# The second MLP's first matrix product in seven block products for eight, its weights prepared step by step behind the first MLP's activations

## The chip, the cores and the metric

The kernel runs on one core of one Trainium2 chip. The metric is the device time of one execution in microseconds (us), the median of several runs. Five engines run side by side, each through its own list of instructions in order: TensorE (PE; PEld is its loading of weights), VectorE (DVE), ScalarE (ACT), GpSimd (POOL) and SyncE (SP), which here issues nearly all transfers (DMAs).

## The reference, cut to what matters

```python
attn_out = _attn_ref(q, k, v, M_prev, z_prev, beta)        # 4 batches, 8 heads, 576 rows, 64 columns
x = attn_out.transpose(0, 2, 1, 3).reshape(2304, 512)      # 2304 tokens
h = x @ moe_w_in                                           # first MLP: 512 -> 2048
x = where(h > 0, h, exp(min(h, 0)) - 1) @ moe_w_out        # ELU, 2048 -> 512
h = x @ moe2_w_in                                          # second MLP: 512 -> 2048
out = maximum(0.01 * h, h) @ moe2_w_out                    # leaky ReLU, 2048 -> 512
```

The weights reach the kernel as 64-bit floats, read as pairs of 32-bit integers.

## The kernel before

**Precision.** PE multiplies numbers of reduced width, so every factor x is held as two parts: the rounded high part `xh` and the rest `xl = x - xh`. A product is the sum of three: high by high, the weights' low by high, high by low. ACT or DVE makes the high part by a rounding copy, POOL (now and then DVE) the low part by a subtraction.

**Stages.** First the attention, with the first MLP's work on hidden blocks 0 to 6 (of 16 blocks of 128 hidden columns) woven into it. Then the rest of the first MLP, hidden blocks 7 to 15, over five token tiles (four of 512, the last of 256); I call it the first MLP's second half. Then the second MLP over the same five tiles.

**The first MLP's second half.** For each tile and each hidden block f: 12 matmuls give the hidden block in a bank of PSUM (`h_mm`, line 621; two banks named `pm` and two named `tp` take turns), `elu` (lines 633 to 635, then `g_split`, lines 243 and 628) passes through ACT twice, DVE twice and POOL once, and 12 matmuls (`o_mm`, line 649) two blocks later add its part of the output, held in four banks named `sc` and `po`. At a tile's end DVE adds the part made beside the attention (line 902) and the result goes to the DRAM scratch `x1_scr`.

**The second MLP's weights.** `load_w` makes one hidden block's weights: two fetches of 0.5 MB, the unpacking of 64-bit floats (ACT line 127, DVE lines 128, 129, 132, each over 128x1024 elements), the rounding copy (ACT line 241) and two subtractions (POOL line 138). A list `w2` holds the sixteen; two per tile are taken from it in tiles 1 to 4 of the first MLP's second half, the others are emitted behind that stage.

**The second MLP.** `load3` fetches a tile's input from `x1_scr` and splits it (ACT, POOL line 840). Each hidden block has 12 matmuls of 512 columns (line 621), `leaky` (ACT line 640, DVE line 641, then `g_split`), and two blocks later 12 matmuls into the output banks (line 919). At a tile's end DVE copies the four output banks in eight halves through two buffers named `st` (line 953), each sent out by its own DMA (line 954). All sixteen blocks' weights stay in SBUF.

**Order.** The code is emitted in this order, but a scheduler with a timeline model of its own sets each engine's list. `tc.issue_after` holds an instruction behind another, and a tile's buffer can be written anew only when its last reader is done.

## Time and profile before

| | us |
|---|---|
| median of 3 runs (1069.12 to 1070.02) | 1069.39 |
| profiled execution | 1069.05 |
| its span, first to last instruction | 1067.2 |
| PE busy in the span | 1040.3 |
| DVE busy | 591.8 |
| POOL busy | 531.6 |
| ACT busy | 485.2 |

The times are of one execution taken by the profiler; the span leaves out 1.85 us around the first and last instruction. Busy shares are averages over stages with different limits, so the stages are read one by one. A matmul's duration in the rows overlaps the next one's; its real cost is the distance between starts.

### The profile page before, as it was taken

The page shows a single profiled execution, that of the slowest core. Times are in us where ns is not written, and L with a number is a line of the kernel's source. Part 1 is how long each engine was busy: PE and PEld are TensorE (multiplying, and loading weights), DVE is VectorE, ACT ScalarE, POOL GpSimd, SP SyncE. Part 2 cuts the span into 40 slices and gives each one's busy share as a digit, 9 for nine tenths or more (in the row PEclk, how much of TensorE's full clock was granted, in tenths as well). Part 3 has the DMA queues.
Part 4 walks back from the last instruction along what each step waited for, and adds up shares of the span by engine and source line. Part 5 has one row for each costly group of instructions (what it writes and reads, how often), then busy time and mean ns, then how long its engine had stood idle before and what let it go on. Part 6 is the DMA issues. An engine that isn't in the chain of part 4 may idle for free.

```text
span 1067.2 us, 17324 instructions
## 1 busy us (share of the span) xinstructions
PE 1040.3 (97%) x5904; PEld 909.9 (85%) x5904; DVE 591.8 (55%) x1380; ACT 485.2 (45%) x1171; POOL 531.6 (50%) x674
## 2 busy tenths in 40 slices
...
GB/s 183 195 150 112 160 142 96 139 166 142 115 128 164 90 113 337 147 223 168 227 232 85 119 1 138 158 119 1 80 1 1 60 20 1 8 33 1 1 40 20
DMA packets 150120, 115.05 MB, mean 108 GB/s; under 512 B 80016, under 2 KB 141456, under 8 KB 150032
## 3 DMA queue, kind: packets, MB, share of 16 engines
...
q8 instruction: 47, 0.77, 0.3%
q14 instruction: 41, 0.34, 0.1%
...
## 4 chain that ended last, share of the span: by engine, by line
PE 80%; DVE 7%; DMA 4%; ACT 3%; issue 2%; POOL 2%; SPq 1%; DVEq 0%; POOLq 0%; ACTq 0%
PE pm L621 18%; PE sc L919 14%; PE tp L621 14%; PE sc L649 7%; PE pm L649 5%; PE po L919 4%; PE tp L457 4%; PE po L524 4%; PE pm L524 2%; PE po L649 2%; PE sc L426 2%; PE sc L428 1%; PE sc L429 1%; POOL w L138 1%; DMA wraw<-in_moe_w_in_dram 1%
## 5 line engine op out<-in xcount | busy, mean ns | idle before, releaser
L628 POOL TENSOR_TENSOR gl<-e,gh 128x512 fp32r<-128x512 f32 (+2 forms) x181 | 200.4, 1111 | 371.9 <-DVE gh L243 267.8
L621 PE MATMUL tp<-xw,w 128*128 128x512 f32 (+1 forms) x504 | 144.6, 367 | 1.7 <-DVE e L635 1.7
L621 PE MATMUL pm<-xw,w 128*128 128x512 f32 (+1 forms) x496 | 142.7, 369 | 1.2 <-ACT w L241 1.2
L919 PE MATMUL sc<-w,gh 128*128 128x512 f32 x448 | 135.9, 390 | 0.0
L451 POOL TENSOR_SCALAR pt<-pt,rs,omg 128x128 f32<-128x128 f32 (+4 forms) x160 | 104.1, 660 | 21.2 <-DVE rs L446 17.2
L621 PEld LDWEIGHTS tp<-xw,w 128*128 128x128 f32 x504 | 91.8, 188 | 18.3 <-DVE e L635 2.2
L621 PEld LDWEIGHTS pm<-xw,w 128*128 128x128 f32 x496 | 90.5, 188 | 17.7 <-ACT w L241 1.6
L436 ACT ACTIVATE pt<-pt,mx 128x128 f32<-128x128 f32 (+4 forms) x160 | 93.3, 585 | 23.2 <-DVE mx L431 21.6
L649 PE MATMUL sc<-gh,w 128*128 128x512 f32 (+2 forms) x438 | 103.2, 340 | 0.2 <-DVE gh L243 0.2
L919 PEld LDWEIGHTS sc<-w,gh 128*128 128x128 f32 x448 | 83.2, 188 | 16.5
L621 PE MATMUL tp<-xv,w 128*128 128x512 f32 (+1 forms) x252 | 92.6, 367 | 0.0
L621 PE MATMUL pm<-xv,w 128*128 128x512 f32 (+1 forms) x248 | 91.4, 369 | 0.0
L640 ACT ACTIVATE e<-pm 128x512 f32<-128x512 f32 (+1 forms) x40 | 22.2, 555 | 144.7 <-PE pm L621 141.7
L138 POOL TENSOR_TENSOR w<-wm,w 128x512 fp32r<-128x512 f32 x50 | 65.8, 1337 | 43.4 <-ACT w L241 39.4
L457 PE MATMUL tp<-ident,pt 128*128 128x128 f32 x480 | 82.0, 276 | 3.0 <-DVE al L250 1.5
L641 DVE TENSOR_TENSOR e<-tp,e 128x512 f32<-128x512 f32 (+1 forms) x40 | 25.5, 637 | 106.8 <-ACT e L640 106.8
L919 PE MATMUL sc<-w,gl 128*128 128x512 f32 x224 | 84.3, 389 | 0.0
L649 PEld LDWEIGHTS sc<-gh,w 128*128 128x128 f32 x438 | 74.6, 188 | 9.1 <-DVE gh L243 0.6
L641 DVE TENSOR_TENSOR e<-pm,e 128x512 f32<-128x512 f32 (+1 forms) x40 | 25.5, 637 | 102.1 <-ACT e L640 102.1
L621 PE MATMUL pm<-xh,w 128*128 128x288 f32 x368 | 79.6, 302 | 1.7 <-ACT xh L610 1.6
L243 DVE CAST gh<-e 128x512 fp32r<-128x512 f32 (+2 forms) x146 | 71.0, 490 | 13.5 <-PE po L919 3.0
L640 ACT ACTIVATE e<-tp 128x512 f32<-128x512 f32 (+1 forms) x40 | 22.2, 554 | 117.4 <-PE tp L621 117.4
...
## 6 DMA issues: line engine op xcount, KB each, us to landing
wraw<-in_moe_w_in_dram SPq DMA_DIRECT2D x32, 512.0 KB, 3.9
wraw<-in_moe_w_out_dram SPq DMA_DIRECT2D x32, 512.0 KB, 4.8
...
x<-x1s SPq DMA_DIRECT2D x9, 512.0 KB, 3.8
...
```

What stands on the lines that cost most here:

```text
L138: nc.gpsimd.tensor_tensor(out=w[:, 1, a], in0=t[:, a], in1=_f(w)[:, 0, a], op=ALU.subtract)
L243: (nc.vector if eng == "V" else nc.gpsimd).tensor_copy(dst, src)
L436: nc.scalar.activation(out=pt[0:m, 0:nk], in_=pt[0:m, 0:nk], func=AF.Exp, scale=-1.0, bias=mx[0:m, last:last + 1], accum_out=self.pd["ss"] ...
L451: nc.gpsimd.tensor_scalar(out=pt, in0=pt, scalar1=rs[0:m, i:i + 1], scalar2=omg[0:m, h:h + 1], op0=ALU.mult, op1=ALU.mult,)
L457: nc.tensor.transpose(dst, self.p[c][:, k0:k0 + kn], ident)
L524: nc.tensor.matmul(po[:, a:b], w, x, start=i == 0, stop=i == len(mms) - 1)
L621: nc.tensor.matmul(ph, wi[:, wj, kc, :], xx[:, kc, :], start=n_mm == 0, stop=n_mm == 11)
L628: nc.gpsimd.tensor_tensor(out=gl, in0=g, in1=_f(gh), op=ALU.subtract)
L640: nc.scalar.mul(t, ph, 0.01)
L641: nc.vector.tensor_tensor(out=t, in0=ph, in1=t, op=ALU.max)
L649: nc.tensor.matmul(py, wo[:, wj, ec * P:(ec + 1) * P], gg, start=opens and f == first and n_mm == 0, stop=closes and f == last and n_mm == 2,)
L919: nc.tensor.matmul(pos[tb], gg[:, tb * P:(tb + 1) * P], wo[:, wj, :], start=f == 0 and n_mm == 0, stop=f == NF - 1 and n_mm == 2,)
```

## The change

The first product of the second MLP, for tiles of 512 tokens, is cut into 2 x 2 blocks: for two hidden blocks (a pair, 256 columns) the weights into A11, A12, A21, A22 (256 inputs by 128 hidden columns each) and the tile's input into B11, B12, B21, B22 (256 inputs by 256 tokens). Instead of eight block products, seven are made (`product`, line 1115: six matmuls of 256 columns each), from A11, A12, A22, four sums of weight blocks (S1 to S4) and seven input blocks (B11, B21, B22, T1 to T4). Their results are added on DVE (`add`, line 1121), in two buffers `c0` and `c1` named `e`; then come the leaky ReLU on DVE (line 1125), the rounding copy on ACT (line 1128) and the low part on POOL (line 834). The 256-token tile keeps the old product.

The weight blocks are made in 33 steps, one behind each ELU of the first MLP's second half, from tile 0 on: per pair the unpacking, the split of the A blocks, the DVE sums, the split of the S blocks, and the same for the second matrix. All is written to DRAM scratch (`wa_scr`, `ws_scr`, `wo_scr`); pairs 0 and 1 also stay in SBUF, pair 4 is fetched early, the rest at the end of that stage. In the second MLP five pairs' A and S blocks fit in SBUF, so three pairs' blocks (2 MB each) are fetched again for each tile (`load_pair`), and the pairs are taken forwards and backwards in turn. The input blocks T1 to T4 are made on DVE when a tile of the first MLP ends, and the first tile's seven blocks are fetched and split during the last tile of the first MLP (`fetch_first`, `split_first`).

```diff
+    def decode(raw, m=None):
+        rw = raw.rearrange("p a n t -> p (a n) t")
+        lw, hw = rw[:, :, 0], rw[:, :, 1]
+        if m is None:
+            m = pools["wst"].tile([P, 2 * DM], I32, tag="wm", bufs=pools["nwm"], name="wm")
+        nc.scalar.activation(out=_f(m), in_=_f(hw), func=AF.Copy, scale=2.0 ** -112)
+        nc.vector.tensor_scalar(out=m, in0=m, scalar1=3, scalar2=None, op0=ALU.logical_shift_left)
+        nc.vector.scalar_tensor_tensor(
+            out=m, in0=lw, scalar=29, in1=m, op0=ALU.logical_shift_right, op1=ALU.bitwise_or
+        )
+        nc.vector.scalar_tensor_tensor(
+            out=m, in0=hw, scalar=-(1 << 31), in1=m, op0=ALU.bitwise_and, op1=ALU.bitwise_or
+        )
+        return _f(m)
...
+    x1_scr = [dram.tile([P, 7 if t + TW <= NT else 2, 2, TW // 2], F32, name=f"x1s{t}") for t in range(0, NT, TW)]
+    NPR = NF // 2
+    NKEEP = 2
+    wa_scr, ws_scr, wo_scr = (
+        [dram.tile([P, 4, 2, 2 * P], F32, name=f"{nm}{i}") for i in range(NPR)] for nm in ("wa", "ws", "wo")
+    )
...
+        pools["elu"] = [hi.ins, lo.ins]
...
+    def sub_lo(out, full, hi):
+        nc.gpsimd.tensor_tensor(out=out, in0=full, in1=hi, op=ALU.subtract)
...
+    def stage():
+        nonlocal n_stage
+        n_stage += 1
+        return n_stage % (NFA - 1)
...
+    def fetch_raw(key):
+        kind, pr = key
+        raw = raws[key] = raw_tile()
+        for j in range(2):
+            f = 2 * pr + j
+            if kind == "in":
+                dst = raw[:, j].rearrange("p (c n) t -> p c (n t)", c=NKC)
+                src = w2i[:, f * 2 * P:(f + 1) * 2 * P].rearrange("(c p) n -> p c n", p=P)
+            else:
+                dst, src = raw[:, j].rearrange("p n t -> p (n t)"), w2o[f * P:(f + 1) * P, :]
+            nc.sync.dma_start(dst, src)
...
+    def unpack(key, ahead):
+        m = None
+        if key[0] == "out":
+            m = w_tile(wpa, NFA - 1).rearrange("p a b n -> p (a b n)")[:, 0:2 * DM].bitcast(I32)
+        full[key] = decode(raws.pop(key), m)
+        if ahead:
+            fetch_raw(ahead)
...
+    SLOTS = [("a", 2, 3), ("a", 4, 5), ("b", 0, 1), ("b", 3, 4), None]
...
+    def split_in(pr, half):
+        t = full["in", pr].rearrange("p (k n) -> p k n", k=4)
+        v = as_blocks(w_tile(wpa, SLOTS[pr][1 + half] if pr < NKEEP else stage()))
+        nc.scalar.copy(v[:, :, 0], t)
+        for k in (0, 2):
+            sub_lo(v[:, k:k + 2, 1], t[:, k:k + 2], _f(v)[:, k:k + 2, 0])
+        nc.sync.dma_start((ws_scr if half else wa_scr)[pr], _f(v))
+        if pr < NKEEP:
+            hold(pr, pr, half, v)
+        if half:
+            return
+        for o, a, b, op in (
+            (3, 2, 3, ALU.add), (2, 0, 2, ALU.subtract), (0, 3, 0, ALU.subtract), (1, 1, 0, ALU.subtract)
+        ):
+            nc.vector.tensor_tensor(out=t[:, o], in0=t[:, a], in1=t[:, b], op=op)
...
+    def split_out(pr):
+        t = full["out", pr].rearrange("p (j n) -> p j n", j=2)
+        wt = w_tile(wpa, pr if pr < NKEEP else stage())
+        copy(E_WH, wt[:, :, 0], t)
+        for j in range(2):
+            sub_lo(wt[:, j, 1], t[:, j], _f(wt)[:, j, 0])
+        if pr < NKEEP:
+            hold_out(pr, wt)
+        else:
+            nc.sync.dma_start(wo_scr[pr], _f(as_blocks(wt)))
...
+    keys = [(kind, i) for i in reversed(range(NPR)) for kind in ("in", "out")]
+    w2 = [lambda: [fetch_raw(key) for key in keys[:2]]]
+    for n, key in enumerate(keys):
+        ahead = keys[n + 2] if n + 2 < len(keys) else None
+        kind, i = key
+        first = lambda key=key, ahead=ahead: unpack(key, ahead)
+        if kind == "in":
+            w2 += [first, lambda i=i: split_in(i, 0), lambda i=i: split_in(i, 1)]
+        else:
+            closing_in = w2.pop()
+            w2 += [lambda a=closing_in, b=first: (a(), b()), lambda i=i: split_out(i)]
...
+    XTAGS = ("xw1", "xv1", "xw0", "xv0")
+    def split_blocks(k, st):
+        nb = st.shape[1]
+        xb = mtile(XTAGS[k], 1, F32R, (NKC, TW)).rearrange("p a n -> p (a n)")
+        xb = xb.rearrange("p (k l c n) -> p k l c n", k=2, l=2, c=2)
+        for i in range(nb):
+            b = xb[:, i]
+            nc.scalar.copy(b[:, 0], st[:, i])
+            (nc.vector if k % 2 else nc.gpsimd).tensor_tensor(
+                out=b[:, 1], in0=st[:, i], in1=_f(b)[:, 0], op=ALU.subtract
+            )
+        return [xb[:, i] for i in range(nb)]
+    def load3(gi):
+        n = 7 if wide[gi][1] == TW else 2
+        got = []
+        for k in range((n + 1) // 2):
+            nb = min(2, n - 2 * k)
+            st = mtile("yx"[k % 2], 1, F32, (2, 2, TN))[:, 0:nb]
+            nc.sync.dma_start(st, x1_scr[gi][:, 2 * k:2 * k + nb])
+            got += split_blocks(k, st)
+        return got
...
+    def fetch_first(k):
+        nb = 4 if k == 0 else 3
+        t = _f(w_tile(wpa, NFA - 1)).rearrange("p a b n -> p (a b n)").rearrange("p (k c n) -> p k c n", k=4, c=2)
+        ahead[k] = t[:, 0:nb]
+        pools["x in"] = nc.sync.dma_start(t[:, 0:nb], x1_scr[0][:, 4 * k:4 * k + nb])
+    def split_first(k):
+        st = ahead[k // 2][:, 2 * (k % 2):(4, 3)[k // 2] if k % 2 else 2]
+        ahead.setdefault("x", []).extend(split_blocks(k, st))
+    def behind_elu(*units):
+        with ExitStack() as order:
+            for ins in pools["elu"]:
+                order.enter_context(tc.issue_after(ins))
+            for u in units:
+                u()
...
+    def load_pair(pr, s, n=2):
+        held.pop(pr, None)
+        for half, scr in enumerate((wa_scr[pr], ws_scr[pr])[:n]):
+            if SLOTS[s]:
+                pool, *slots = SLOTS[s]
+                v = as_blocks(w_tile(wpa if pool == "a" else wpb, slots[half]))
+            else:
+                t = raw_tile().rearrange("p a n t -> p (a n t)").bitcast(F32R)
+                v = t.rearrange("p (k l n) -> p k l n", k=4, l=2)
+            nc.sync.dma_start(_f(v), scr)
+            hold(pr, s, half, v)
+    FIRST = {
+        0: [lambda: load_pair(4, 4), lambda: fetch_first(0)],
+        3: [lambda: split_first(0)],
+        4: [lambda: split_first(1)],
+        5: [lambda: fetch_first(1)],
+    }
...
-            if gi >= 1 and f - NFA in (W2A, W2B) and len(w2) > NF - NFA:
-                w2.pop(0)()
+            if gi + 1 == len(wide) and f - NFA in FIRST:
+                behind_elu(*FIRST[f - NFA])
+            elif w2 and not wun:
+                behind_elu(w2.pop(0))
...
+        b11, b12, b21, b22 = (y[:, :, o:o + w // 2] for y in ys for o in (0, w // 2))
+        for k, x in ((0, b11), (1, b21), (3, b22)):
+            nc.sync.dma_start(x1_scr[gi][:, k], x)
+        for k, o, a, b in ((2, b11, b12, b11), (6, b12, b22, b12), (4, b22, b22, b11), (5, b21, b21, b22)):
+            nc.vector.tensor_tensor(out=o, in0=a, in1=b, op=ALU.subtract)
+            nc.sync.dma_start(x1_scr[gi][:, k], o)
...
+    for k in (2, 3):
+        split_first(k)
+    cur = ahead["x"]
+    with tc.issue_after(pools["y in"].ins), tc.issue_after(pools["x in"].ins):
+        load_pair(2, 2)
+        fetch_out(2, wpb, 2)
+        load_pair(3, 3)
+        fetch_out(3, wpb, 5)
+        for pr in range(4, 7):
+            fetch_out(pr, wpb, pr + 2)
+        fetch_out(7, wpa, 6)
...
+        seq = list(range(NPR))[::-1 if gi % 2 else 1]
+        fs = [2 * pr + j for pr in seq for j in range(2)]
...
+        def product(wb, xb):
+            out = h_bank()[:, 0:h]
+            for kc in range(2):
+                for n, (a, b) in enumerate(((0, 0), (1, 0), (0, 1))):
+                    nc.tensor.matmul(
+                        out, wb[:, a, kc, :], xb[:, b, kc, :], start=kc == n == 0, stop=kc == 1 and n == 2
+                    )
+            return out
...
+        def rows(f, c):
+            flat = c.rearrange("p a n -> p (a n)")
+            nc.vector.scalar_tensor_tensor(out=flat, in0=flat, scalar=0.01, in1=flat, op0=ALU.mult, op1=ALU.max)
+            gh = mtile("gh", NG, F32R)[:, 0:w]
+            gl = mtile("gl", NG, F32R)[:, 0:w]
+            nc.scalar.copy(gh, flat)
+            sub_lo(gl, flat, _f(gh))
+            gs[f] = gh, gl
...
+            slot, (a11, a12, _, a22), (s2, s4, s3, s1) = held[pr]
+            b11, b21, t1, b22, t2, t4, t3 = cur
+            c0, c1 = (mtile("e", EB)[:, 0:w].rearrange("p (a n) -> p a n", a=2) for _ in range(2))
+            u, d = c1[:, 0], c1[:, 1]
+            nc.scalar.copy(u, product(a11, b11))
+            add(c0[:, 0], product(a12, b21), u)
+            nc.scalar.copy(d, product(s1, t1))
+            add(c0[:, 1], product(s4, b22), d)
+            add(u, product(s2, t2), u)
+            add(c0[:, 1], c0[:, 1], u)
+            rows(2 * pr, c0)
+            if n:
+                emit_o3(fs[2 * n - 2])
+            add(u, product(s3, t3), u)
+            add(d, d, u)
+            add(u, product(a22, t4), u)
+            rows(2 * pr + 1, c1)
+            if n < 3:
+                load_pair(seq[n + 5], slot)
+            if n:
+                if n == NPR - 1:
+                    cur = load3(gi + 1)
+                emit_o3(fs[2 * n - 1])
```

How the change moves instructions, at three places. PE in the second MLP, away from a tile's ends, before: the tail of one hidden block's 12 matmuls (`tp`, inputs `xw` and `xv`) and the 12 output matmuls of an earlier one (`sc`, `po`).

```order
L621 MATMUL tp<-xw_9026,w_8918 128x512 x2
L621 MATMUL tp<-xv_9027,w_8918 128x512
L621 MATMUL tp<-xw_9026,w_8918 128x512 x2
L621 MATMUL tp<-xv_9027,w_8918 128x512
L919 MATMUL sc<-w_8448,gh 128x512 x2
L919 MATMUL sc<-w_8448,gl 128x512
L919 MATMUL sc<-w_8448,gh 128x512 x2
L919 MATMUL sc<-w_8448,gl 128x512
L919 MATMUL sc<-w_8448,gh 128x512 x2
L919 MATMUL sc<-w_8448,gl 128x512
L919 MATMUL po<-w_8448,gh 128x512 x2
L919 MATMUL po<-w_8448,gl 128x512
```

The same place after the change, in tile 1: the fourth product of a pair, half of an earlier block's output matmuls, the fifth product, the other half, the sixth and seventh product.

```order
L1115 MATMUL pm<-xv_9949,w_10098 128x256 x6
L1101 MATMUL sc<-w_9198,gh 128x512 x2
L1101 MATMUL sc<-w_9198,gl 128x512
L1101 MATMUL sc<-w_9198,gh 128x512 x2
L1101 MATMUL sc<-w_9198,gl 128x512
L1115 MATMUL tp<-xw_9956,w_10098 128x256 x6
L1101 MATMUL sc<-w_9198,gh 128x512 x2
L1101 MATMUL sc<-w_9198,gl 128x512
L1101 MATMUL po<-w_9198,gh 128x512 x2
L1101 MATMUL po<-w_9198,gl 128x512
L1115 MATMUL pm<-xv_9963,w_10098 128x256 x6
L1115 MATMUL tp<-xw_9956,w_10096 128x256 x6
```

The unit between two uses of the PSUM banks `pm` and `tp` has shrunk from 12 matmuls of 512 columns to 6 of 256, and output matmuls stand between the products at three points of a pair. DVE at the start of a tile of the second MLP, before: the copies of the last tile's output banks (`st`) stand between the leaky ReLUs (`e`) and rounding copies (`gh`) of the new tile.

```order
L953 COPY st<-sc 128x256 x2
L641 TENSOR_TENSOR e<-pm,e 128x512
L243 CAST gh<-e 128x512
L953 COPY st<-sc 128x256 x2
L641 TENSOR_TENSOR e<-tp,e 128x512
L953 COPY st<-sc 128x256
L243 CAST gh<-e 128x512
L953 COPY st<-sc 128x256
L953 COPY st<-po 128x256
L641 TENSOR_TENSOR e<-pm,e 128x512
L953 COPY st<-po 128x256
L243 CAST gh<-e 128x512
```

After the change, at the start of tile 1, the copies stand between the adds that empty the products' banks.

```order
L1121 TENSOR_TENSOR e<-tp,e 128x256
L1191 COPY st<-sc 128x256 x2
L1121 TENSOR_TENSOR e<-tp,e 128x256
L1191 COPY st<-sc 128x256 x2
L1121 TENSOR_TENSOR e<-pm,e 128x256
L1121 TENSOR_TENSOR e<-e 128x256
L1125 SCALAR_TENSOR_TENSOR e<-e 128x512
L1121 TENSOR_TENSOR e<-tp,e 128x256
L1191 COPY st<-sc 128x256 x2
L1121 TENSOR_TENSOR e<-e 128x256
L1121 TENSOR_TENSOR e<-pm,e 128x256
L1125 SCALAR_TENSOR_TENSOR e<-e 128x512
```

The copies, which wait for the DMAs that empty `st`, now stand ahead of adds for which PE's next products wait. PE at the same place after the change, from the fourth product of tile 1's first pair to the fifth of its second (the nine output matmuls on `w_9206` are this tile's first).

```order
L1115 MATMUL tp<-xv_9949,w_9468 128x256 x6
L1115 MATMUL pm<-xw_9956,w_9468 128x256 x6
L1115 MATMUL tp<-xv_9963,w_9468 128x256 x6
L1115 MATMUL pm<-xw_9956,w_9466 128x256 x6
L1115 MATMUL tp<-xw_9942,w_9368 128x256 x6
L1115 MATMUL pm<-xw_9942,w_9368 128x256 x6
L1115 MATMUL tp<-xv_9949,w_9370 128x256 x6
L1101 MATMUL sc<-w_9206,gh 128x512 x6
L1115 MATMUL pm<-xv_9949,w_9370 128x256 x6
L1101 MATMUL sc<-w_9206,gl 128x512 x3
L1115 MATMUL tp<-xw_9956,w_9370 128x256 x6
```

Seven products follow each other there with no output matmul between. POOL in the last tile of the first MLP's second half, before: low parts of ELUs (`gl`), of weights (`w`) and of the second MLP's first input tile (`xv`).

```order
L628 TENSOR_TENSOR gl<-e,gh 128x256 x4
L138 TENSOR_TENSOR w_8918<-wm,w_8918 128x512 x2
L840 TENSOR_TENSOR xv_9027<-x,xw_9026 128x256 x4
L628 TENSOR_TENSOR gl<-e,gh 128x256 x3
L138 TENSOR_TENSOR w_8930<-wm,w_8930 128x512 x2
L840 TENSOR_TENSOR xv_9027<-x,xw_9026 128x256 x4
L628 TENSOR_TENSOR gl<-e,gh 128x256 x2
```

After the change: the last weight blocks (`w_8688`, `w_8773`, `w_8730`, pair 0's) among the tile's nine ELUs, then input blocks 0 and 1 (`xw_8973`), two ELUs, and blocks 4 and 5 (`xw_9180`).

```order
L834 TENSOR_TENSOR w_8688<-wm,w_8688 128x2x256 x2
L641 TENSOR_TENSOR gl<-e,gh 128x256
L834 TENSOR_TENSOR w_8773<-w_8735,w_8773 128x512 x2
L641 TENSOR_TENSOR gl<-e,gh 128x256 x2
L834 TENSOR_TENSOR w_8730<-wm,w_8730 128x2x256 x2
L641 TENSOR_TENSOR gl<-e,gh 128x256 x4
L956 TENSOR_TENSOR xw_8973<-w_8878,xw_8973 128x512 x2
L641 TENSOR_TENSOR gl<-e,gh 128x256 x2
L956 TENSOR_TENSOR xw_9180<-w_9049,xw_9180 128x512 x2
```

The split of input blocks 4 and 5, which the fifth and seventh product of the second MLP's first pair read, is the last thing that POOL does before that pair's own low parts.

## Rows read from the trace of the kernel before

**Rows 1.** Busy time by stretch: engine busy (instructions), granted clock, DMA share, GB/s.

```profile
core 0: us, PE busy (x) PEld busy (x) DVE busy (x) ACT busy (x) POOL busy (x), PEclk, DMA share, GB/s
500.00:525.00 25.00, 25.00 (x112) 20.72 (x111) 20.39 (x24) 13.36 (x19) 16.83 (x12) 1.00 0.89 292
550.00:675.00 125.00, 125.00 (x654) 107.89 (x654) 48.55 (x74) 41.62 (x75) 50.28 (x44) 1.00 0.32 101
680.00:1020.00 340.00, 340.00 (x1510) 281.95 (x1510) 99.44 (x170) 56.08 (x98) 116.17 (x100) 1.00 0.10 32
1020.00:1062.00 42.00, 42.00 (x269) 38.07 (x268) 13.23 (x38) 5.78 (x15) 11.82 (x16) 1.00 0.06 20
```

**Rows 2.** Waits of PE, 425 to 680 us: total, times, longest.

```profile
PE tp L621 <- DVE e L635: 1.7, 1, 1.7
PE pm L621 <- ACT w L241: 1.2, 1, 1.2
PE sc L649 <- DVE gh L243: 0.2, 1, 0.2
```

**Rows 3.** Chain that ended last: start, us, engine, tile, line, matmuls.

```profile
697.00 2.72 PE pm L621 x12
...
833.00 2.72 PE tp L621 x12
```

**Rows 4.** PE in order of time, one hidden block of the 256-token tile.

```profile
1046.07 0.40 PE L621 MATMUL tp<-xw,w 128*128 128x256 f32 x2
...
1047.50 0.63 PE L919 MATMUL sc<-w,gh 128*128 128x512 f32 x2
...
1048.89 0.40 PE L621 MATMUL pm<-xw,w 128*128 128x256 f32 x2
```

**Rows 5.** ACT groups, 440 to 700 us: count, busy, mean ns, idle before.

```profile
L634 ACT ACTIVATE e<-e 128x512 f32<-128x512 f32 x36 | 22.5, 632 | 1.0
L127 ACT ACTIVATE wm<-wraw 128x1024 f32<-128x1024 f32 x18 | 20.5, 1140 | 39.2 <-POOL w L138 37.7 <-DMA x<-ys 1.4
L241 ACT CAST w<-wm 128x1024 fp32r<-128x1024 f32 x18 | 18.9, 1051 | 34.8 <-DVE wm L132 34.3 <-PE po L649 0.5
```

**Rows 6.** DVE groups, 440 to 700 us.

```profile
L129 DVE SCALAR_TENSOR_TENSOR wm<-wraw,wm 128x1024 int32<-128x1024 int32 x18 | 29.0, 1610 | 0.5
L243 DVE CAST gh<-e 128x512 fp32r<-128x512 f32 x42 | 26.4, 634 | 2.4 <-PE po L649 0.3
L132 DVE SCALAR_TENSOR_TENSOR wm<-wraw,wm 128x1024 int32<-128x1024 int32 x18 | 22.7, 1261 | 0.3
L128 DVE TENSOR_SCALAR wm<-wm 128x1024 int32<-128x1024 int32 x18 | 15.4, 857 | 35.5 <-ACT wm L127 35.5
L635 DVE SCALAR_TENSOR_TENSOR e<-e,tp 128x512 f32<-128x512 f32 x18 | 12.3, 684 | 31.6 <-ACT e L634 30.1 <-POOL gl L628 1.6
```

**Rows 7.** POOL groups, 440 to 700 us.

```profile
L628 POOL TENSOR_TENSOR gl<-e,gh 128x512 fp32r<-128x512 f32 x41 | 57.4, 1406 | 81.9 <-PE po L649 41.3 <-DVE gh L243 29.6 <-PE tp L621 9.5
L138 POOL TENSOR_TENSOR w<-wm,w 128x512 fp32r<-128x512 f32 x37 | 48.6, 1335 | 39.1 <-ACT w L241 35.1 <-PE po L649 4.0
```

**Rows 8.** DVE in order of time, two unpacking steps.

```profile
442.67 1.23 DVE L129 SCALAR_TENSOR_TENSOR wm<-wraw,wm 128x1024 int32<-128x1024 int32 x1
...
504.84 2.20 DVE L129 SCALAR_TENSOR_TENSOR wm<-wraw,wm 128x1024 int32<-128x1024 int32 x1
```

**Rows 9.** DVE and ACT groups of the 256-token tile, 1020 to 1062 us.

```profile
L641 DVE TENSOR_TENSOR e<-tp,e 128x256 f32<-128x256 f32 x8 | 3.4, 425 | 12.6 <-ACT e L640 12.6
...
L640 ACT ACTIVATE e<-tp 128x256 f32<-128x256 f32 x8 | 3.1, 385 | 17.6 <-PE tp L621 17.6
```

**Rows 10.** POOL group, 800 to 1000 us.

```profile
L628 POOL TENSOR_TENSOR gl<-e,gh 128x512 fp32r<-128x512 f32 x37 | 47.8, 1292 | 137.9 <-DVE gh L243 137.9
```

**Rows 11.** DVE in order of time at a tile's start, with its waits.

```profile
766.13 0.42 DVE L953 COPY st<-sc 128x256 f32<-128x256 f32 x1 [0.89 <-DMA out_dram<-st]
...
768.38 0.42 DVE L953 COPY st<-po 128x256 f32<-128x256 f32 x1 [1.16 <-DMA out_dram<-st]
```

**Rows 12.** DMA queue, 500 to 600 us: packets, MB, share of 16 engines.

```profile
q1 hardware_dynamic: 17721, 18.84, 58.1%
```

**Rows 13.** DMA issues of the page: count, KB each, us to landing.

```profile
x<-x1s SPq DMA_DIRECT2D x9, 512.0 KB, 3.8
```

127 lines of the change are left out of this document (71 added, 56 removed).

## The prediction

> **What bounds the kernel now.** I read the stretches of busy time first. In both MLP stages PE is busy for the whole of each stretch, at a granted clock of 1.00 (the 2.4 GHz level), also in the 256-token tile, while DVE, ACT and POOL stay far below it [rows 1]. Then the waits: between 425 and 680 us PE lost 3.1 us, twice nearly all of it to one wait each, on DVE and on the split of a weight [rows 2]. Then the chain that ended last: from 697.00 to 833.00 it is PE alone, twelve matmuls in 2.72 us and again twelve [rows 3]; 25 hidden blocks of 24 matmuls lie between, so a block costs 136.00/25 = 5.44 us and a 512-column matmul 0.2267. So the time of both stages is PE's number of columns, and what the other engines do costs nothing as long as it stays hidden. The profiled execution took 1069.05 us (span 1067.2 and 1.85 around it), 0.34 below the median.
>
> **The products.** The nearest row for 256 columns is the 256-token tile: from 1046.07 to 1047.50 twelve such matmuls, with the same change of weights between them, took 1.43 us, 0.119 each; the six of 512 columns behind them 1.39 against 6 x 0.2267 = 1.36, so 0.03 for a switch of kind [rows 4]. A pair of hidden blocks had 48 x 0.2267 = 10.88 us. It gets 42 x 0.119 = 5.00 for seven products, 24 x 0.2267 = 5.44 for the unchanged output matmuls and three switches, 0.10: 10.54. The gain is 0.34 us a pair; 8 pairs in 4 tiles make 32 x 0.34 = **10.9 us**. The bound on that side, with no switch cost, is 0.44 x 32 = 14.1.
>
> The Trainium skill ("TensorE: Matmul & The Clock Gate", section "Back-to-back issue gap") speaks against the change: in a real stream, it says, weight load and matmul set the spacing together, 81 ns at 128 columns and 131 at 512. A straight line gives 98 ns at 256 (an estimate from that page), so a pair would cost 42 x 98 + 24 x 131 = 7.26 us for 48 x 131 = 6.29, a loss of 31 us in all. The trace has 119 and 227 ns, nearly one to two, so I go by the rows.
>
> **Tile starts, the new wait.** Inside a tile a pair's results go through a loop: the second buffer `c1` is free for the next pair's first result only when the pair's last add (0.425), its leaky ReLU (0.684), the rounding copy (0.632) and POOL's low part (1.292) are done, and the fifth product needs the bank that ACT's copy (0.385) then empties: 3.4 us [rows 5, 6, 9, 10]. PE meanwhile has twelve output matmuls, four products (4 x 0.714) and six output matmuls: 2.72 + 2.86 + 1.36 = 6.94 us. So nothing waits there, with 3.5 us to spare for hand-overs. At a tile's start the first pair has no output matmuls, seven products stand in a row, and DVE copies the old banks in between, in eight pieces of 0.42 us; with two buffers a second piece into the same buffer comes 2.25 us after the first (766.13 to 768.38, with waits of 0.89 and 1.16 for the DMAs) [rows 11]. I follow the two engines by the order's rows, from the end of the old tile's output matmuls as time 0. DVE makes two copies by 0.84, an add, and two more by 3.1, held by the DMA. Then come the adds and leaky ReLUs: fifth product's add to 3.5, the sum and the ReLU to 4.6, the sixth's add to 5.06. PE could start the third product of the next pair at about 4.5, but its bank is the sixth's: 0.56 us lost. The first output matmuls need the low part of the first row, ready at 4.6 + 0.63 + 1.29 = 6.55, while PE is through at 5.78: 0.77 lost. Two more copies put the `c1` loop's end at 9.75, while PE is through at 9.3: 0.45 lost. Together 1.8 us in each of three tiles. The first tile has no copies ahead of it; the same sum without them gives no wait, and I put 0.4. That makes **5.8 us**; low end 0 (DVE's copies taken between), high end 2.8 a tile, if the hand-overs that no row prices add 1 us, 8.8.
>
> **The junction of the MLPs.** The first tile's last three input blocks (0.79 MB) are fetched into the staging buffer that the first four leave, once these are split on ACT, POOL and DVE; then blocks 4 and 5 pass POOL (1.335 each) before the fifth product. From the fifth ELU of the last tile PE has about three blocks of 2.82 us [rows 4] and four products of 0.714, some 11 us; the split takes 2.7, the fetch over 3.8 (that is for 0.5 MB [rows 13]) and the second split 2.0, behind POOL's ELUs. It about closes. Bounds: 0, and a whole fetch and a split, 5.1. I take **1.0**.
>
> **The weights, first MLP's second half.** POOL's, DVE's and ACT's work doubles here. A pair of keys, four ELUs or 4 x 5.44 = 21.76 us of PE, adds on DVE two unpackings (0.857 + 1.610 + 1.261 = 3.73 each) and four sums of 0.43: with the ELUs' 4 x 1.32 it makes 14.5 us, 66%. POOL has six low parts of 1.335 and four of 1.406, 13.6 us, 63%; ACT two of 1.140, three of 1.051 and eight of 0.632, 10.5 us, 48% [rows 5 to 7]. Is that covered? From 500 to 525 us DVE was busy 20.39, POOL 16.83 and ACT 13.36 of 25 us, denser on all three, and PE had 25.00 [rows 1]. A chain that is serial could still bind: a key's unpacking, split, sums and second split make 1.14 + 3.73 + 1.05 + 2.67 + 1.72 + 1.05 + 2.67 = 14.0 us; with the slower unpacking (2.20 for 1.61 [rows 8]), sums at 0.684 and an ELU's instruction ahead of each of the seven steps (3 x 0.632, 2 x 0.684, 2 x 1.406 = 6.1) it is 21.7, as long as the 21.76 in which the four steps must be taken. Cover is there, but thin; with hand-overs the high end is 0.75 over in each of eight pairs, 6. Low end 0. I take **0.5**, nearer to the dense window.
>
> **Transfers.** In that half, by the tiles' sizes, 16.8 MB of raw weights, 23.1 of scratch writes and 21.7 of the MLP's own and of early loads move in 36 x 5.44 + 9 x 2.82 = 221 us, 279 GB/s. The queue did 18.84 MB in 100 us at 58.1%, which is 324 GB/s at full [rows 12]. In the second MLP three pairs (6.3 MB) per tile of 84 us are 75 GB/s, asked for three pairs ahead. I cost both at nothing; without the early request a pair would wait several times the 3.8 us that 0.5 MB takes [rows 13].
>
> **The sum:** 1069.05 - 10.9 + 5.8 + 1.0 + 0.5 = 1065.45, and 0.34 for the median: **1065.8 us**. By the ends of the terms the forecast itself lies between 1062 and 1069.
>
> **Rivals.** (A) The starts and the junction cost nothing, since DVE's copies fall into gaps: 1059. For it: DVE is busy 99 of 340 us in the second MLP [rows 1]. Against: its instructions are taken in order, and the copies stand ahead. Chance 0.20. (B) The weight chain or the junction takes its high end, about +5: 1071, no change; the chain's 21.7 of 21.76 speaks for it, the dense window against. 0.12. (C) Slower: the `c1` loop binds in every pair, since hand-overs and POOL's low part take over 3.5 us more than the 3.4 summed. At 0.8 us in each of the 28 pairs that follow another, 22 us: 1088. It decides from 0.13 us a pair (3.6/28 undoes the gain), and is measurably slower from 0.20. Nothing in the rows is that long; but PE has four banks for seven products. 0.14. (D) DVE and POOL shut each other out. The same unpacking took 1.23 us alone and 2.20 beside POOL [rows 8]; fully serial, 14.5 + 13.6 = 28.1 us stand against 21.76, +6.3 in eight pairs: 1116. Against it: 37.2 us of both in 25 [rows 1]. 0.02. The Trainium skill ("SBUF — State Buffer", section "SBUF: two separate sides") has that rule, an exclusive lock of the shared port for a whole instruction; the 1.23 against 2.20 agrees with it in part. (E) Weight loads pace the small matmuls: PE's loads were busy 38.07 us for 268 at the end [rows 1], 0.142 each; 42 of these in place of 0.119 add 0.97 a pair, 31 us: 1097. The twelve in 1.43 us speak against it. 0.01. The Trainium skill's section cited above has such a rule. (F) A small matmul costs less than in the short tile, say half of 0.2267, and switches nothing: 0.68 a pair, 22 us saved where I have 10.9: 1055. 0.01. That the change doesn't do what it says is excluded by the order: 42 matmuls of 256 columns a pair.
>
> **How the numbers follow.** The forecast holds 0.50. A measurement of this kernel tells 0.2%, 2.1 us, from no change: faster is below 1067.2, slower above 1071.5. Of the forecast's 0.50 some 0.38 lie below 1067.2; with A and F faster has 0.59. Slower has C, D, E and a quarter of B, 0.20; the rest, 0.21, is no change. The range runs from 1057, under A, to 1074, above B, and leaves out most of C, D, E and F.
>
> **What would show it.** Products: starts of the seven products' matmuls 0.119 apart, a pair 10.54 us from first product to first product away from tile ends. Starts: PE waits on DVE's adds, then on POOL's low part and ACT's copy, 1.8 us a tile. Junction: a wait of the fifth product on the POOL split, 1 us. Weights: PE's waits of 3.1 us in that half hardly grow. The prediction is wrong if the pair is not 10.54, if PE waits in every pair on ACT's first copy, or if ELU waits on DVE or POOL appear from 450 to 680 us.

## The result, and the profile after

The changed kernel takes 1079.72 us (median of 5 runs, 1079.21 to 1082.01), the kernel before 1069.12 beside it: a ratio of 1.0100, 95% interval 1.0086 to 1.0114. I had forecast 1065.8; it is slower by 10.6 us.

I read the trace after in the same order. First the stretches of busy time around the first MLP's second half (500 to 700 us; the first line is the stretch of [rows 1]).

```profile
core 0: us, PE busy (x) PEld busy (x) DVE busy (x) ACT busy (x) POOL busy (x), PEclk, DMA share, GB/s
...
500.00:525.00 25.00, 22.48 (x98) 17.99 (x97) 22.45 (x27) 12.31 (x19) 14.64 (x11) 1.00 0.90 327
500.00:650.00 150.00, 139.85 (x605) 112.54 (x604) 128.60 (x142) 64.55 (x86) 96.27 (x65) 1.00 0.86 314
650.00:700.00 50.00, 44.38 (x316) 40.73 (x316) 36.34 (x56) 19.95 (x40) 32.01 (x26) 1.00 0.84 299
```

Before, PE had 125.00 of 125.00 us in the middle of that half [rows 1]. Now it has 139.85 of 150, with DVE at 128.60 and POOL at 96.27, and 44.38 of the next 50. From 700 us on the trace lists no wait of PE. The waits say where, from 440 to 700 us:

```profile
PE sc L665 <- DVE gh L256: 5.3, 4, 2.0
PE sc L665 <- POOL gl L641: 5.1, 5, 1.8
PE tp L634 <- DVE e L649: 4.1, 3, 1.7
...
PE tp L1115 <- ACT xv L955: 0.5, 1, 0.5
PE pm L1115 <- POOL xw L956: 0.3, 1, 0.3
PE pm L1115 <- ACT xw L955: 0.3, 1, 0.3
```

With three others (1.4, 1.2 and 0.2) they make 18.4 us in place of 3.1 [rows 2], 14.5 of them for ELU results (`gh`, `gl`, `e`). Each wait costs a little more than its length: a matmul alone behind a wait has 0.50 us in its row (at 545.47) where one in a row has 0.39, and it overlaps none before it. From 500 to 600 us there are 397 matmuls where the kernel before has 443, and 46 x 0.2267 = 10.4 us, while PE idles 8.0 in seven waits. To size the whole loss I take the end of the first MLP on PE, in order of time:

```profile
685.78 0.88 PE L1115 MATMUL pm<-xw,w 128*128 128x256 f32 x6
686.50 0.88 PE L1115 MATMUL tp<-xw,w 128*128 128x256 f32 x6
687.22 0.76 PE L1115 MATMUL pm<-xv,w 128*128 128x256 f32 x5
...
690.58 0.28 PE L665 MATMUL po<-gl,w 128*128 128x256 f32 x1
```

Its last output matmul starts at 690.58, and 17 matmuls of the second MLP (6, 6 and 5, 0.119 each, 2.0 us) have run by then: 688.6. In the kernel before the last one starts at 674.93, with 24 of the second MLP's 512-column matmuls (5.44 us) ahead of it: 669.5. So the first MLP ends **19.1 us later**. The second MLP, by the second product of tiles 1 and 2 (that of tile 3 starts at 944.10):

```profile
774.99 0.88 PE L1115 MATMUL tp<-xw,w 128*128 128x256 f32 x6
...
859.54 0.88 PE L1115 MATMUL tp<-xw,w 128*128 128x256 f32 x6
```

84.55 us a tile for 8 x 10.88 = 87.04 [rows 3]: 10.0 us in four tiles are won, tile starts included. The junction costs 0.54 + 0.31 + 0.29 = 1.1 us of waits. 1069.05 - 10.0 + 19.1 + 1.1 = 1079.3, against 1080.18 for the profiled execution; 0.9 us I can't place.

Why does the ELU come late? The groups of DVE from 500 to 650 us (count, busy, mean ns, idle before):

```profile
L896 DVE TENSOR_TENSOR wm<-wm 128x256 f32<-128x256 f32 x28 | 21.9, 781 | 4.4 <-POOL w L834 4.0
L256 DVE CAST gh<-e 128x512 fp32r<-128x512 f32 x26 | 20.7, 800 | 0.9
...
L649 DVE SCALAR_TENSOR_TENSOR e<-e,tp 128x512 f32<-128x512 f32 x13 | 8.9, 681 | 7.2 <-ACT e L648 7.2
```

A sum of weight blocks, 128x256, takes 0.781 us, where an add of that size took 0.425 [rows 9]; a rounding copy 0.800 for 0.634 [rows 6]; the twelve differences of input blocks take 1.0 to 1.7 (0.68 to 1.01 in lows_dve, a later run). The ELU's own step that reads PSUM (`e<-e,tp`) takes its 0.681 as before (0.684 [rows 6]). What lengthens the others is seen in order of time, DVE first, then POOL:

```profile
503.73 0.41 DVE L256 CAST gh<-e 128x512 fp32r<-128x512 f32 x1
504.06 1.51 DVE L896 TENSOR_TENSOR wm<-wm 128x256 f32<-128x256 f32 x1
505.50 1.51 DVE L256 CAST gh<-e 128x512 fp32r<-128x512 f32 x1
506.93 3.40 DVE L896 TENSOR_TENSOR wm<-wm 128x256 f32<-128x256 f32 x3
...
503.77 2.96 POOL L834 TENSOR_TENSOR w<-w,w 128x512 fp32r<-128x512 f32 x2
506.69 2.90 POOL L641 TENSOR_TENSOR gl<-e,gh 128x512 fp32r<-128x512 f32 x2
```

The rounding copy at 503.73, which starts ahead of POOL's subtraction of 503.77, takes 0.41 us. The sum at 504.06 takes 1.51 and the copy at 505.50 1.51, and each ends shortly behind one of POOL's two subtractions (the second ends at 506.73, the copy at 507.01). Three more sums take 3.40 beside POOL's next two. So in these rows a DVE instruction whose inputs all lie in SBUF waits inside itself for POOL, and the wait counts as busy time.

The Trainium skill ("SBUF — State Buffer", section "SBUF: two separate sides") says that DVE and GpSimd share a port pair as an exclusive lock for a whole instruction, and that it concerns DVE's two-port modes and operations with two inputs in SBUF. The trace agrees, 0.41 against 1.51 and 0.681 against 0.684 for the step with an input in PSUM.

Some of the delay reaches PE through ACT, though ACT is busy for only 64.55 of the 150 us. PE at 513 us, ACT ahead of it, and ACT's group of weight copies from 500 to 650 us:

```profile
513.41 0.74 PE L634 MATMUL tp<-xw,w 128*128 128x512 f32 x2 [1.69 <-DVE e L649]
```

```profile
510.36 1.05 ACT L885 CAST w<-wm 128x1024 fp32r<-128x1024 f32 x1 [6.67 <-DVE wm L896]
```

```profile
L885 ACT CAST w<-wm 128x1024 fp32r<-128x1024 f32 x14 | 14.7, 1052 | 36.2 <-DVE wm L896 20.8 <-DVE wm L102 15.3
```

The hidden block for which PE waits here was complete in its bank at about 506.3 (its last matmul starts at 505.89), but the ELU's first step on ACT starts only at 511.31: it stands behind the weight copy, for which ACT had idled 6.67 us until the lengthened sums on DVE were done. ACT idles 36.2 us in front of such copies.

### The profile page after: what moved, and what is told of

The parts are those of the page before. It is cut to its first block, busy times and chain, and to the rows that moved or that the text cites. A ratio compares the mean times of both kernels' runs of the same rounds, so it can differ in the third digit from the quotient of the medians.

```text
span 1078.4 us, 19007 instructions
## 1 busy us (share of the span) xinstructions
PE 1035.9 (96%) x6480; PEld 927.9 (86%) x6480; DVE 744.5 (69%) x1600; ACT 521.9 (48%) x1237; POOL 558.6 (52%) x672
## 4 chain that ended last, share of the span: by engine, by line
PE 74%; DVE 12%; issue 4%; ACT 3%; DMA 3%; POOL 2%; SPq 2%; DVEq 0%; POOLq 0%; ACTq 0%
PE sc L1101 14%; PE pm L634 8%; PE pm L1115 7%; PE tp L1115 7%; PE sc L665 5%; PE pm L665 5%; PE po L1101 4%; PE po L537 4%; PE tp L470 4%; PE tp L634 4%; PE pm L537 2%; PE sc L441 2%; PE sc L442 2%; PE sc L439 1%; DVE gh L256 1%
## 5 line engine op out<-in xcount | busy, mean ns | idle before, releaser
L834 POOL TENSOR_TENSOR gl<-e,gh 128x512 fp32r<-128x512 f32 x64 | 82.6, 1291 | 226.6 <-ACT gh L1128 205.2
L641 POOL TENSOR_TENSOR gl<-e,gh 128x288 fp32r<-128x288 f32 (+2 forms) x117 | 117.5, 1009 | 118.7 <-DVE gh L256 64.9
L1128 ACT CAST gh<-e 128x512 fp32r<-128x512 f32 x64 | 39.7, 620 | 187.4 <-DVE e L1125 187.2
L444 DVE CUSTOM_DVE_ANT_0 pt<-sc,mask 128x128 f32<-128x128 f32 (+4 forms) x160 | 69.3, 444 | 7.8 <-PE sc L442 3.8
L665 PE MATMUL sc<-gl,w 128*128 128x512 f32 (+2 forms) x219 | 66.3, 344 | 5.1 <-POOL gl L641 5.1
L470 PEld LDWEIGHTS tp<-ident,pt 128*128 128x128 f32 x480 | 59.7, 143 | 9.8 <-ACT ah L260 2.1
L665 PE MATMUL pm<-gh,w 128*128 128x288 f32 x280 | 63.3, 307 | 0.0
L634 PEld LDWEIGHTS pm<-xh,w 128*128 128x128 f32 x368 | 60.1, 191 | 2.0 <-ACT xh L623 1.8
L634 PE MATMUL tp<-xw,w 128*128 128x512 f32 (+1 forms) x184 | 53.2, 368 | 4.1 <-DVE e L649 4.1
L634 PE MATMUL pm<-xl,w 128*128 128x288 f32 x184 | 55.8, 304 | 0.0
```

What stands on the lines that cost most here:

```text
L444: nc.vector.tensor_tensor_reduce(out=pt[0:m, k0:k0 + n], in0=sc[0:m, 0:n], in1=mk, op0=ALU.add, op1=ALU.min, scale=-0.125, scalar=mx[0:m, ...
L470: nc.tensor.transpose(dst, self.p[c][:, k0:k0 + kn], ident)
L634: nc.tensor.matmul(ph, wi[:, wj, kc, :], xx[:, kc, :], start=n_mm == 0, stop=n_mm == 11)
L641: lo = nc.gpsimd.tensor_tensor(out=gl, in0=g, in1=_f(gh), op=ALU.subtract)
L665: nc.tensor.matmul(py, wo[:, wj, ec * P:(ec + 1) * P], gg, start=opens and f == first and n_mm == 0, stop=closes and f == last and n_mm == 2,)
L834: nc.gpsimd.tensor_tensor(out=out, in0=full, in1=hi, op=ALU.subtract)
```

## The experiments

Theory 1, formed from this profile: DVE and POOL lengthen each other, and the ELU's steps queue behind the weights' on both. Rivals: POOL's low parts of the weights stand ahead of the ELU's low part (2); the input blocks' differences at tile ends (3); a step that holds both a split and the next unpacking (4). The table has, from 500 to 650 us, the idle time of PE and the busy times of DVE and POOL (from the windows, as above).

| run | median us | ratio to before (95%) | PE idle | DVE | POOL |
|---|---|---|---|---|---|
| before | 1069.12 | | 0.0 | 72.9 | 57.9 |
| changed kernel | 1079.72 | 1.0086 to 1.0114 | 10.2 | 128.6 | 96.3 |
| no_weight_sums | 1072.17 | 1.0021 to 1.0049 | 6.6 | 119.9 | 112.6 |
| no_input_sums | 1080.90 | 1.0093 to 1.0126 | 7.8 | 117.2 | 95.1 |
| elu_cast_on_act | 1075.86 | 1.0050 to 1.0080 | 7.4 | 109.1 | 97.6 |
| no_weight_lows | 1069.94 | 0.9990 to 1.0010 | 2.8 | 114.9 | 40.7 |
| no_sums_no_lows | 1070.99 | 1.0004 to 1.0023 | 5.8 | 100.1 | 42.3 |
| act_sums_pool | 1080.74 | 1.0083 to 1.0125 | 9.1 | 95.4 | 120.2 |
| spread_39 | 1083.59 | 1.0111 to 1.0150 | 10.2 | 126.9 | 96.1 |
| lows_dve | 1071.39 | 1.0008 to 1.0027 | 4.4 | 139.7 | 52.0 |
| **act_lows_dve** | **1063.34** | **0.9926 to 0.9960** | 1.5 | 135.4 | 44.5 |
| before_act | 1070.44 | 1.0000 to 1.0019 | 0.0 | 54.5 | 56.3 |
| lows_memset | 1073.14 | 1.0020 to 1.0043 | 1.8 | 123.1 | 59.7 |

**no_weight_sums**

```diff
-            nc.vector.tensor_tensor(out=t[:, o], in0=t[:, a], in1=t[:, b], op=op)
+            pass
```

> The changed kernel without the four DVE sums per pair of weight blocks (the S blocks are then split from the unsummed blocks; 32 instructions left out). Theory 1: the first MLP's second half waits because DVE is full, its unpacking and sums standing ahead of the ELU's instructions and stretched by POOL beside them. Then 25 us of DVE work gone (28 of the sums took 21.9 us between 500 and 650 us) takes most of PE's 15 us of new waits there: 1066 to 1072 us. Rival 2: POOL's low parts of the weights stand ahead of the ELU's low part; then the sums matter little: 1076 to 1080. Rival 3: the sums of the input blocks at the tiles' ends are what delays; then also 1076 to 1080.

1072.17: the sums are worth 7.5 us, at the end of what theory 1 gave, so rivals 2 and 3 are not the whole. DVE and POOL together are busier than in the changed kernel (232.4 us for 224.9), and yet PE waits less.

**no_input_sums**

```diff
-            nc.vector.tensor_tensor(out=o, in0=a, in1=b, op=ALU.subtract)
```

> The changed kernel without the four DVE differences that make the input blocks T1 to T4 at a tile's end (16 instructions left out; the transfers stay, and carry unsubtracted blocks). Rival 3: six of the PE waits over 0.7 us start within 20 us of a tile's end, so about half of the loss goes: 1070 to 1074 us. Theory 1: they are 4 x 5.4 = 22 us of the same full DVE and give back their share, 3 to 6 us: 1074 to 1077. Rival 2: nothing, 1078 to 1080.

1080.90, no gain; theory 1 and rival 3 missed, and it lies just above rival 2's range. PE's idle time from 500 to 650 us does fall, to 7.8, but the junction takes it back, in one wait whose chain shows the fetch of the first tile's last three blocks:

```profile
PE pm L1114 <- ACT xw L955: 4.8, 1, 4.8
```

```profile
684.29 1.72 POOL xw L956
...
686.02 5.14 DMA w<-x1s
```

The fetch waits for POOL's split of the first blocks and then takes 5.14 us: the high end that the prediction had given the junction. The differences' cost by themselves stays open.

**elu_cast_on_act**

```diff
-    E_GH, ... = "V", ...
+    E_GH, ... = "A", ...
```

> The changed kernel with the ELU's rounding copy on ACT in place of DVE in the first MLP's second half (and in the short tile of the second MLP); nothing is left out. Theory 1: DVE loses 26 x 0.80 = 20.7 us of 150 between 500 and 650 us, ACT, at 44%, gains 26 x 0.63 = 16 us: PE's waits there fall to some 5 us, 1066 to 1072. Rival 2: POOL's queue is unchanged, 1077 to 1081. Against both: ACT's queue could become the next wait, since its weight copies of 1.05 us stand ahead.

1075.86, 3.9 us won, between the two ranges: DVE falls by 19.5 us, but the sums left on it get longer still (1.007 us each), with POOL as busy as before.

**no_weight_lows**

```diff
-        for k in (0, 2):
-            sub_lo(v[:, k:k + 2, 1], t[:, k:k + 2], _f(v)[:, k:k + 2, 0])
+        nc.scalar.copy(v[:, :, 1], t)
```

(and the same in `split_out`)

> The changed kernel with the low parts of the second MLP's weights left out on POOL: in each step one rounding copy on ACT (1.05 us) writes that half of the tile in place of two POOL subtractions (3.0 us). Rival 2: POOL's queue was the cause, and with 72 us of POOL work gone the waits go: 1063 to 1067 us. Theory 1: POOL's part is only that it stretches DVE's instructions beside it (sums of 0.78 us against 0.43); the sums and casts become shorter, DVE's load falls from 86% to some 75%, and about half of the loss goes: 1069 to 1074. Rival 3: 1078 to 1080.

1069.94, 9.8 us won, as theory 1 had it. DVE's list is the same, yet its rounding copies come down from 0.800 to 0.583 us. Not at 1063 to 1067, as rival 2 had it; part of the rest is the edit's own, as the next run shows.

**no_sums_no_lows**: both edits.

> The changed kernel without the four sums per pair of weight blocks and with the low parts of these weights written by a rounding copy on ACT in place of POOL's subtractions: both earlier omissions in one. Theory 1 (DVE and POOL together are too full in the first MLP's second half, each lengthening the other): DVE falls to some 100 of 150 us, POOL to 40, PE waits no more there than before the change, and what is left of the change is the second MLP's gain of 84.55 against 87.04 us a tile, 10.0 us, less a little at the junction: 1060 to 1063 us. Rival: a part of the waits comes from the steps' places, two unpackings in one step and their transfers, which this kernel keeps: 1065 to 1069 us.

1070.99, neither the 1060 to 1063 of theory 1 nor the rival's 1065 to 1069. PE's waits, the clock, and ACT in order of time:

```profile
PE tp L634 <- DVE e L649: 7.4, 2, 5.8
```

```profile
505.00:510.00 5.00, 1.58 (x4) 1.29 (x5) 2.92 (x4) 3.08 (x5) 0.00 (x0) 0.76 1.05 372
510.00:515.00 5.00, 5.00 (x15) 3.88 (x14) 3.00 (x4) 3.40 (x4) 3.40 (x2) 0.56 1.05 415
```

```profile
499.28 1.06 ACT L885 CAST w<-wm 128x1024 fp32r<-128x1024 f32 x1 [2.49 <-DVE wm L102]
...
502.14 1.04 ACT L886 CAST w<-wm 128x1024 fp32r<-128x1024 f32 x1
...
506.94 1.14 ACT L648 ACTIVATE e<-e 128x512 f32<-128x512 f32 x2
```

One wait of 5.8 us at 508 makes all of the idle time: without the sums four weight copies of 1.05 us stand in a row on ACT from 499.28 to 503.18, ahead of the ELU's first step (503.08), and two more copies and an unpacking step (504.05 to 507.05) ahead of its second step at 506.94. Three of the six copies were put there by the edit (the run before has a wait of 2.8 us at the same place). While PE waits, and behind the wait, its granted clock falls to 0.76 and 0.56, that is in part to its lower level of 1.2 GHz; from 510 to 515 PE is busy throughout at 0.56, which loses another 5 x 0.44 = 2.2 us (an estimate). So the two omissions do not show theory 1's floor; apart from this one wait PE is not idle from 500 to 650 us.

**act_lows_dve**: the ELU's copy on ACT, and

```diff
-            sub_lo(v[:, k:k + 2, 1], t[:, k:k + 2], _f(v)[:, k:k + 2, 0])
+            nc.vector.tensor_tensor(out=v[:, k:k + 2, 1], in0=t[:, k:k + 2], in1=_f(v)[:, k:k + 2, 0], op=ALU.subtract)
```

(and the same in `split_out`)

> Nothing left out: the ELU's rounding copy on ACT, as in the run before, and the weights' low parts on DVE in place of POOL, so that POOL has only the ELU's low parts. If what hurts is that DVE and POOL lengthen each other (a rounding copy takes 0.80 us beside a busy POOL and 0.58 beside an idle one), DVE loses 29 us of stretch and 11 of copies and gains 40 x 0.68 = 27 of 150 us, and the time falls below that with the copy alone: 1069 to 1074 us. If it is only the amount of work in DVE's list, DVE gets fuller than with the copy on ACT alone: 1077 to 1084 us.

1063.34: faster than both kernels, 0.57% below the one before, and below what I gave theory 1. Its window and all of PE's waits from 440 to 700 us:

```profile
500.00:650.00 150.00, 148.52 (x662) 121.45 (x662) 135.38 (x172) 85.78 (x124) 44.45 (x29) 1.00 0.95 342
```

```profile
PE sc L665 <- ACT gh L255: 1.1, 3, 0.5
PE tp L634 <- DVE e L649: 1.1, 2, 0.8
PE pm L634 <- ACT w L255: 0.4, 1, 0.4
PE sc L665 <- DVE x L1057: 0.2, 1, 0.2
```

DVE is busier than in the changed kernel, 135.38 for 128.60, and carries 45 of POOL's former instructions there (0.757 us each for the 31 of the first matrix, 1.000 for the 14 of the second); PE waits 2.8 us. The DMA share is 0.95 for 0.86, so the scratch traffic was not what held it. The first MLP ends, counted as above, 3.4 us later than before instead of 19.1.

**act_sums_pool**: the ELU's copy on ACT, the weight blocks' sums by `nc.gpsimd` in place of `nc.vector`.

> Nothing left out: the ELU's rounding copy on ACT and the weight blocks' sums on POOL in place of DVE. If only DVE's list is too long, it loses 20 to 28 us of 150 more and the time falls to 1068 to 1072 us. If the two engines share a resource and their sum counts, POOL gains as much or more (32 x 0.7 us) in front of the ELU's low parts, and it is no better than the 1075.9 of the copy alone: 1074 to 1079 us.

1080.74, 4.9 us slower than with the copy alone and above both ranges: DVE is emptied to 95.4 us, POOL filled to 120.2 (a sum takes 1.019 us there), and PE waits for POOL.

```profile
PE sc L665 <- POOL gl L641: 8.0, 10, 1.8
```

A theory in which DVE's list alone is too long falls here.

**spread_39**

```diff
-            w2 += [lambda a=closing_in, b=first: (a(), b()), lambda i=i: split_out(i)]
+            w2 += [lambda a=closing_in, b=first: (a(), b())] if i > 5 else [closing_in, first]
+            w2.append(lambda i=i: split_out(i))
```

> Nothing left out: six of the eight steps that hold the second split of a pair's blocks and the unpacking of the next key are cut in two, 39 steps for 33, the last of them in the short tile. If the double steps make PE's waits (two of DVE's waits at 503 and 513 us, 2.5 us, stand behind two unpackings side by side), 1073 to 1077 us. If only the total of the work counts, 1078 to 1081 us, and it can be slower if the steps in the short tile delay the junction of the MLPs.

1083.59, slower. This does not settle rival 4, since up to 608 us nothing moved: the lists of DVE, ACT and POOL are those of the changed kernel to there, and PE has the same waits. The wait at 513.41 shown above is here:

```profile
514.04 0.73 PE L634 MATMUL tp<-xw,w 128*128 128x512 f32 x2 [1.69 <-DVE e L649]
```

The two waits named in the expectation belong to pair 7, the first that is unpacked (DVE from 495 and from 497 us), and the edit leaves pairs 7 and 6 as they were. What the run shows is that steps in the short tile delay the junction:

```profile
PE tp L1116 <- DVE e L1122: 2.9, 1, 2.9
```

Against rival 4 speak lows_dve and act_lows_dve, which keep the double steps: most of PE's waits go in act_lows_dve all the same.

**lows_dve**: the weights' low parts on DVE, the ELU's copy there too.

> Nothing left out: the weights' low parts on DVE in place of POOL, the ELU's rounding copy stays on DVE. DVE gets 40 x 0.7 = 28 us of work more between 500 and 650 us, on top of 128.6 of 150, if its instructions keep their length. If the number of instructions in its list decides, PE waits more than in the changed kernel: 1084 to 1092 us. If DVE's and POOL's instructions lengthen each other, POOL's quiet gives back about as much (29 us, worked out from casts of 0.80 against 0.41, sums of 0.78 against 0.43 and unpackings of 1.7 against 1.2), and PE waits for POOL no more: 1066 to 1072 us.

1071.39, 8.3 us faster than the changed kernel with its fullest engine busy for 11 us more. The three groups that tell it, DVE's and POOL's:

```profile
L256 DVE CAST gh<-e 128x512 fp32r<-128x512 f32 x28 | 14.3, 510 | 1.7 <-PE po L665 0.7
L896 DVE TENSOR_TENSOR wm<-wm 128x256 f32<-128x256 f32 x28 | 13.6, 487 | 0.1
```

```profile
L641 POOL TENSOR_TENSOR gl<-e,gh 128x512 fp32r<-128x512 f32 x28 | 52.9, 1893 | 100.8 <-DVE gh L256 94.0 <-PE tp L634 4.1 <-PE sc L665 2.6
```

Rounding copies 0.510 for 0.800, sums 0.487 for 0.781; POOL, which has only the ELU's low parts left, now takes 1.893 for 1.512: the lengthening goes both ways. PE's waits for the copy `gh`, 5.3 us in the changed kernel, are gone, though DVE's list is longer; those for `gl` fall from 5.1 to 3.2, those for `e` rise from 4.1 to 5.4. The four kernels of copy and low parts give 1079.7, 1075.9, 1071.4 and 1063.3: the copy on ACT is worth 3.9 us with the low parts on POOL and 8.1 with them on DVE.

**before_act**: the kernel before with the rounding copy on ACT.

> The kernel before with the rounding copy of the ELU and of the leaky ReLU on ACT in place of DVE, behind the attention; nothing left out. A control: PE waits there for 3.1 us in all, so no more than that can be won, and the version with the copy and the weights' low parts moved has its lead from the seven products: 1067 to 1070 us. If instead the copy on ACT were worth as much by itself, 1063 to 1065.

1070.44 (1069.88 for the kernel before beside it): the copy's place alone wins nothing before, so the lead of act_lows_dve is not the copy's.

**lows_memset**

```diff
-            sub_lo(v[:, k:k + 2, 1], t[:, k:k + 2], _f(v)[:, k:k + 2, 0])
+            nc.gpsimd.memset(_f(v)[:, k:k + 2, 1], 0.0)
```

(and the same in `split_out`)

> The changed kernel with POOL's subtractions for the weights' low parts replaced by as many memsets of zero on POOL, which write the same 128x512 halves and read nothing (the low parts are left out so); DVE's and ACT's lists keep their work. If DVE and POOL lengthen each other when both read from SBUF, DVE's sums and rounding copies come down from 0.78 and 0.80 us to about the 0.49 and 0.51 that they took with the low parts on DVE, and the time to 1064 to 1070 us. If POOL's memsets hold DVE up as its subtractions did, the DVE durations stay, and so does the time within what the shorter memsets give POOL's own queue: 1073 to 1080 us.

1073.14, at the low end of the second range, while the durations lie between the two theories (0.628 for a sum, 0.703 for a rounding copy). Two places in order of time say more, DVE first:

```profile
546.72 1.67 DVE L256 CAST gh<-e 128x512 fp32r<-128x512 f32 x1
...
549.02 2.19 DVE L99 SCALAR_TENSOR_TENSOR wm<-wraw,wm 128x1024 int32<-128x1024 int32 x1
...
545.05 2.13 POOL L641 TENSOR_TENSOR gl<-e,gh 128x512 fp32r<-128x512 f32 x1 [8.24 <-DVE gh L256]
547.13 0.98 POOL L887 MEMSET w<- 128x512 f32 x2
548.56 1.57 POOL L641 TENSOR_TENSOR gl<-e,gh 128x512 fp32r<-128x512 f32 x1 [0.45 <-DVE gh L256]
550.08 0.99 POOL L887 MEMSET w<- 128x512 f32 x2
```

The subtraction beside which the rounding copy starts ends at 547.18, but the copy ends at 548.39, so its own 0.42 us began only when the two memsets were about through (548.11): the memsets hold it too. The unpacking ends at 551.21, so its own 1.22 began at 549.99, when the subtraction of 548.56 was nearly through, and it ran beside the memsets: they do not hold it. The Trainium skill ("SBUF — State Buffer", section "SBUF: two separate sides") makes the same distinction: operations with two inputs in SBUF are locked out only by a GpSimd operation that reads SBUF. This one pair of rows agrees. PE idles only 1.8 us here from 500 to 650. Most of its waits, 12.4 us from 440 to 720, lie outside, above all one of 2.9 us at 484 and one of 4.1 at 666.

## Why the prediction was wrong

**The products** held. Away from a tile's ends a pair took the 10.54 us worked out, here from first product to first product:

```profile
801.57 0.88 PE L1115 MATMUL tp<-xw,wraw 128*128 128x256 f32 x6
...
812.11 0.88 PE L1115 MATMUL pm<-xw,w 128*128 128x256 f32 x6
```

On the mean of a tile it is 10.57 (84.55/8), and 10.0 us are won in all, tile starts included: the row of the short tile was the right price.

**Tile starts**: 5.8 us was mis-sized. 84.55 - 8 x 10.54 = 0.23 a tile, 0.9 in four. The seven products run one behind the other; at the start of tile 1, behind them:

```profile
782.38 1.55 PE L1101 MATMUL sc<-w,gh 128*128 128x512 f32 x6
783.94 0.98 PE L1115 MATMUL pm<-xv,w 128*128 128x256 f32 x6
784.76 0.86 PE L1101 MATMUL sc<-w,gl 128*128 128x512 f32 x3
```

I had the first output matmuls wait for the low part (6.55 us from time 0, at 776.75). But the six at 782.38 read the high part alone, and the three that read `gl` come at 784.76, behind a product. The order's rows in front of me showed that. The other two waits of the sum (0.56 and 0.45) don't show either: DVE's eight copies come in four pairs, at 776.34, 778.67, 781.25 and 788.91, 0.74 to 0.81 us a pair, and no wait for a DMA stands ahead of any.

**The junction** held in its number, 1.1 us of waits for 1.0, and partly by luck: 0.83 of it is for ACT's copies, where the prediction had named POOL's split alone; that has 0.31. In no_input_sums the same place cost 4.8.

**The weights** are the step that failed: "Cover is there, but thin ... I take 0.5", with a high end of 6. It cost 19.1 us: DVE and POOL hold each other's instructions up, and the ELU's steps stand behind the weights' steps in the lists, so that its results come late. Two things were wrong. I priced the added instructions at the mean durations of a stretch in which POOL was less busy (a sum at 0.43, measured 0.781; a rounding copy at 0.634, measured 0.800), and left the tile ends' differences (twelve from 500 to 650 us, 16.3 us) out of DVE's 66%; it was 86%. And I took one window of 25 us as proof of cover. There DVE and POOL together had (20.39 + 16.83)/25 = 1.49 of the time [rows 1], in the changed kernel (128.60 + 96.27)/150 = 1.50. That it lasts longer is not what made the difference: in the same 25 us the changed kernel has (22.45 + 14.64)/25 = 1.48, and PE already waits there, 0.83 and 1.69 us. So a dense window without a wait proved nothing about other work of the same density. In the one wait followed above the order of the steps made it; no run changes the order alone, so its share stays open.

**The range** was also narrower than the terms. With all high ends the sum is 1069.39 - 10.9 + 8.8 + 5.1 + 6 = 1078.4, where the forecast's upper end was put at 1069.

**Transfers** cost nothing that the runs show: act_lows_dve, with the same traffic in less time, ends the first MLP 3.4 us late.

**The rivals.** By its time C (1088) came nearest, but its loop did not bind: the trace lists no wait of PE from 700 us on. By its mechanism D did, that DVE and POOL shut each other out, at a chance of 0.02 and a price of 51 us; rows 8, the same unpacking in 1.23 and 2.20 us, were its evidence. It acts for part of the instructions only, so its price lay between 0 and that, and such a middle should have carried most of the chance. lows_dve and act_lows_dve, which move work onto the busier of the two engines and win 8.3 and 16.4 us, show that the two hold each other up and that most of the loss hangs on what stands on which of them. How the 19.1 us divide between instructions made longer and queues made longer (rival 2 among them) is not settled, since each experiment changed both.
